# Loading the first token tile in two halves, its first weights on ScalarE's queue, and running its matmuls ahead of the second tile's

## The chip, the cores and the metric

The kernel runs on one core of a Trainium2 chip. The metric is the device time of one execution in microseconds (us). The profile is of one execution; a time of the kernel is the median of several runs without it. The core has TensorE (PE in the profile; its weight loads are PEld), VectorE (DVE), ScalarE (ACT), GpSimd (POOL) and SyncE (SP). SP and ACT issue the DMAs here, each into a queue of its own; the transfers of both queues run on the core's 16 DMA engines. In the trace a DMA is a short issue on SP or ACT, and it is over when its semaphore is full, which the profile calls its landing.

## The reference

Two attention blocks work on the same tokens x (2048 tokens of 1024 features, bfloat16), and a gate per token mixes them. Block A is linear attention with 32 heads of 32; block B is a dilated sliding window of 8 keys, 2 apart. Both project x with a 1024x3072 matrix, and both end in a 1024x1024 matrix.

```
g = sigmoid((x * gate_w).sum(-1))
a = A_ref(x, A_wqkv, A_wo)      # phi(q) (phi(k)^T v) / (phi(q) sum phi(k)), then @ wo
b = B_ref(x, B_wqkv, B_wo)      # softmax over 8 keys at distance 0, 2, .. 14, then @ wo
out = g * a + (1 - g) * b
```

What matters here is the first thing that the kernel computes: V of block B, that is x @ B_wqkv[:, 2048:3072].

## The kernel before, in words

The function plan() records every operation with P.op: its engine, an estimated cost, the tiles that it reads and writes, and a priority. P.schedule() then lays the operations out engine by engine with a small list scheduler (of what is ready, the lowest priority number first), and emit() writes each engine's instructions in that order, with semaphore waits where a dependence crosses engines or goes through a DMA. So a row's place in an engine's program is the planner's; on the chip each engine works through its rows in order, and one that waits holds up all behind it. plan() is run six times (PASSES), each time with the release times of the PSUM banks of the pass before, and the plan with the shortest estimated span is kept.

The tokens are cut in 16 tiles of 128. A token tile is needed transposed, features on the partitions: load_x (line 1334) issues one DMA transpose on SP for a tile, which fills xT[:, 0:8, tile], 8 groups of 128 features. The matmuls of a tile are 8 per half of V: each takes one feature group of the tile as its stationary operand (LDWEIGHTS reads xT) and streams 512 columns of the weights ws[0] past it, and the 8 add up in one PSUM bank. load_w (line 1339) loads a range d0 to d1 of the feature groups of one 512-column half of the weights: the first half comes in four pieces of two feature groups each, here called w0 to w3, of 256 KB each; the second half also comes in four pieces.

The V stage is written out in the list steps (lines 1417 to 1425). Each entry is (tile, half, first feature group, last). Before the change the first half goes

```
cuts = [(0, 4), (4, 6), (6, 8)] if half == 0 else [(0, 2), (2, 4), (4, 6), (6, 8)]
steps += [[(i, half, lo, hi) for i in range(2)] for lo, hi in cuts]
```

so tile 0 takes feature groups 0 to 3, then tile 1 the same ones, then both take 4 and 5, then both 6 and 7; tiles 2 and 3 follow whole; then the second half of the four tiles; then tiles 4 to 15, both halves of a feature group under one weight load (two, line 1363). group (line 1371) makes the matmuls of one entry. Where a group waits for a piece, all of PE waits. The results leave PSUM by move (line 1399) on ACT or DVE into one of 8 slots of vst, and SP stores them in HBM (line 1447).

Ahead of all this stand WARM small matmuls on constants into PSUM bank 7 (line 1410), which need no data and keep PE running while the first loads are under way.

Banks come from pools. In the V stage main holds banks 0 to 6. Then, at line 1472, main becomes banks 0 to 3, for all that follows until line 1824: K and Q of block B (lines 1605 to 1621: the first 1024 tokens, then the others) and the window attention, whose scores are in banks 4 to 7 and which starts when the first 1024 tokens of K and Q are done.

## Time and profile before

| what | value |
|---|---|
| median of 3 runs | 477.44 us (476.99 to 477.62) |
| the profiled execution | 477.52 us |
| its span in the profile | 475.7 us |
| PE busy in the span | 467.0 us, 98% |
| first matmul on data of the kernel | 6.20 us after the span's start |
| TensorE clock granted | 1.0 of full speed over the profile's slices |

The span is the time from the first to the last instruction in the profile; 1.8 us of the execution lie outside of it. PE is busy in all slices of the span, so time is read at PE: where its string of matmuls breaks, and what ended the break. At the start that is the arrival of x and of the weights. In the rows of instructions the first number is the start in us from the span's start, the second the time from the first start to the last end, xN the number of instructions in the row, and in square brackets the idle time of that engine ahead of it and what ended it.

### The profile page before, as it was taken

The numbers are of one execution on the slowest core, as the hardware profiler recorded it, in microseconds if no ns is written. First come the engines' busy times: TensorE is split into PE (matmuls) and PEld (weight loads), VectorE is DVE, ScalarE is ACT, GpSimd is POOL, SyncE is SP. The second block draws the span as 40 slices with busy tenths as digits, with TensorE's granted clock in tenths as the row PEclk, the third lists the DMA queues.
The fourth block names the chain that finished last, engine by engine and source line by source line (L and its number), as shares of the span: only waits on it lengthen the run. The fifth ranks groups of instructions, "written<-read, shape, count | busy, mean of one in ns | idle before, by whom it ended". The sixth has DMA issues, their size and how long they took to land.

```text
span 475.7 us, 9166 instructions
## 1 busy us (share of the span) xinstructions
PE 467.0 (98%) x3988; PEld 210.7 (44%) x3890; DVE 313.0 (66%) x554; ACT 130.1 (27%) x175; POOL 40.2 (8%) x39
## 2 busy tenths in 40 slices
PE   9999999999999999999999999999999999999997
PEld 2322244444445544454444544544444444444444
DVE  2121365799877888878864464589987777777522
ACT  2111112222243535556543423153221111111000
POOL 3000000000000000000068651010000000000000
PEclk9999999999999999999999999999999999999999
DMA  8999997332211253255325866671331111121111
GB/s 223 223 194 296 359 341 234 82 95 57 78 34 53 69 165 88 75 145 142 77 69 150 195 157 104 173 218 24 90 88 47 45 44 45 58 76 47 45 45 48
DMA packets 94969, 57.07 MB, mean 120 GB/s; under 512 B 55240, under 2 KB 88392, under 8 KB 94920
## 3 DMA queue, kind: packets, MB, share of 16 engines
q1 hardware_dynamic: 94088, 55.61, 43.6%
q10 hardware_dynamic: 832, 0.79, 0.6%
q8 instruction: 33, 0.54, 0.5%
q14 instruction: 16, 0.13, 0.1%
HBM read 30.56 MB, written 12.72 MB: 91 GB/s over the span
## 4 chain that ended last, share of the span: by engine, by line
PE 93%; DVE 3%; DMA 2%; issue 1%; POOL 0%; ACT 0%; DVEq 0%
PE ps_all L1375 46%; PE ps_all L1804 23%; PE ps_all L1733 11%; PE ps_all L1360 6%; PE ps_all L1366 4%; PE ps_all L1533 2%; PE ps_all L1560 1%; DMA z_hbm<-zc 1%; DMA zr<-z_hbm 1%; DVE p L1384 1%; DVE prod L1779 0%; DVE den L1780 0%; POOL zb L1687 0%; DVE kT L1402 0%; DVE pn L1784 0%
## 5 line engine op out<-in xcount | busy, mean ns | idle before, releaser
L1375 PE MATMUL ps_all<-xT,w 128*128 128x512 bf16 x500 | 110.2, 379 | 1.2 <-issue 0.8
L1375 PEld LDWEIGHTS ps_all<-xT,w 128*128 128x128 bf16 x512 | 49.6, 98 | 59.5 <-issue 0.3
L1381 ACT ACTIVATE e<-ps_all 128x512 bf16<-128x512 f32 x64 | 38.2, 597 | 125.1 <-PE ps_all L1375 116.2
L1375 PE MATMUL ps_all<-w,xT 128*128 128x512 bf16 x312 | 69.0, 379 | 1.1 <-DVE e L1382 1.0
L1804 PE MATMUL ps_all<-kT,aT 128*128 128x512 bf16 (+1 forms) x259 | 60.2, 372 | 0.3
L1804 PE MATMUL ps_all<-w,qT 128*128 128x512 bf16 (+1 forms) x255 | 59.7, 372 | 0.8 <-DVE p L1384 0.4
L1375 PE MATMUL ps_all<-kT,xT 128*128 128x512 bf16 x254 | 57.6, 379 | 0.3 <-issue 0.2
L1733 PE MATMUL ps_all<-pk,xn 128*128 128x512 bf16 x249 | 55.0, 379 | 1.1 <-issue 1.1
L1375 PEld LDWEIGHTS ps_all<-w,xT 128*128 128x128 bf16 x320 | 30.6, 98 | 41.5 <-DMA w<-in_B_wqkv_dram 5.5
L1405 DVE TENSOR_SCALAR o<-ps_all,gm 128x512 bf16<-128x512 f32 (+1 forms) x28 | 20.5, 732 | 28.1 <-PE ps_all L1804 27.6
L1804 PEld LDWEIGHTS ps_all<-w,qT 128*128 128x128 bf16 x264 | 25.7, 98 | 29.9 <-DVE p L1384 0.5
L1804 PEld LDWEIGHTS ps_all<-kT,aT 128*128 128x128 bf16 x264 | 25.8, 98 | 29.4
L1402 DVE CAST vst<-ps_all 128x512 bf16<-128x512 f32 x16 | 10.5, 690 | 42.8 <-PE ps_all L1360 31.5
L1375 PEld LDWEIGHTS ps_all<-kT,xT 128*128 128x128 bf16 x256 | 24.6, 98 | 29.9 <-issue 0.5
L1733 PEld LDWEIGHTS ps_all<-pk,xn 128*128 128x128 bf16 x256 | 24.5, 98 | 28.7
L1382 DVE TENSOR_SCALAR e<-e 128x512 bf16<-128x512 bf16 x64 | 18.8, 294 | 27.9 <-ACT e L1381 27.5
L1360 PE MATMUL ps_all<-w,xT 128*128 128x512 bf16 x96 | 36.4, 379 | 0.2
L1541 ACT ACTIVATE E<-ps_all 128x1824 bf16<-128x1824 f32 (+1 forms) x18 | 30.4, 1688 | 20.4 <-PE ps_all L1560 18.8
L1366 PE MATMUL ps_all<-w,xT 128*128 128x512 bf16 x92 | 34.9, 379 | 0.0
L1697 POOL TENSOR_TENSOR zacc<-zacc,pk 128x1024 f32<-128x1024 f32 x15 | 33.0, 2198 | 11.8 <-DVE E L1546 10.9
L1575 DVE TENSOR_TENSOR ao<-ps_all,rs 128x896 bf16<-128x896 f32 (+1 forms) x36 | 24.5, 684 | 0.2
L1403 ACT ACTIVATE kT<-ps_all 128x512 bf16<-128x512 f32 x26 | 15.0, 598 | 35.4 <-PE ps_all L1375 35.4
(69 smaller groups left out, 405.2 us busy)
## 6 DMA issues: line engine op xcount, KB each, us to landing
v<-vB_hbm SPq DMA_DIRECT2D x36, 132.0 KB, 3.2
vB_hbm<-vst SPq DMA_DIRECT2D x32, 132.0 KB, 6.3
w<-in_B_wqkv_dram SPq DMA_DIRECT2D x4, 1024.0 KB, 8.5
xt<-in_A_x_dram SPq DMA_DIRECT2D x16, 256.0 KB, 4.3
w<-in_A_wqkv_dram SPq DMA_DIRECT2D x4, 1024.0 KB, 9.3
xn<-in_A_x_dram SPq DMA_DIRECT2D x8, 512.0 KB, 4.9
out_dram<-o SPq DMA_DIRECT2D x15, 256.0 KB, 2.0
oB_hbm<-ao SPq DMA_DIRECT2D x32, 114.0 KB
```

Of the source, the lines that this page charges most:

```text
L1360: return e.add_instruction(mybir.InstMatmult(name=nc.get_next_instruction_name(), engine=mybir.EngineType.PE, ins=[e.lower_ap(rhs), e.lowe ...
L1366: e.matmul(bs[0].ap(), lhs(dc), rhs[0](dc), start=(dc == 0), stop=(dc == 7))
L1375: last = e.matmul(bank.ap(), lhs(dc), rhs(dc), start=(dc == 0), stop=(dc == 7))
L1381: P.op("act", lambda e: e.activation(e_[:, :], bank.ap(), ACT.Exp), act(512), reads=[bank.iv], writes=[e_.all()])
L1382: P.op("dve", lambda e: e.tensor_scalar(e_[:, :], e_[:, :], 1.0, 1e-6, op0=ALU.min, op1=ALU.add), 0.25, reads=[e_.all()], writes=[e_.all()])
L1403: fa = lambda e: e.activation(dst, src(), ACT.Copy)
L1405: fd = lambda e: e.tensor_scalar(dst, src(), scale, None, op0=ALU.mult)
L1541: P.op("act", lambda e: e.activation(E[:, 0:32 * nq].rearrange("p (j q) -> p j q", j=4), ps[:, 4:8, 0:8 * nq], ACT.Exp), act(32 * nq), rea ...
L1575: P.op("dve", lambda e, i0=i0, i1=i1, src=src: e.tensor_tensor(o_[:, :, i0:i1, :], src(0, 32), rs[:, :, i0:i1, None].to_broadcast([128, 2, ...
L1697: P.op("pool", lambda e, t=t: e.tensor_tensor(zacc[:, :], zacc[:, :], pkS[:, t, :], ALU.add), 2.2, reads=[src, zacc.all()], writes=[zacc.a ...
L1733: last = e.matmul(bank.ap(), tl[:, t, cs:cs + 128], pkS[:, t, r * 512:(r + 1) * 512], start=(t == 0), stop=(t == NT - 1))
L1804: last = e.matmul(bank.ap(0, f1 - f0), lh[:, k, t * 128:(t + 1) * 128], w[:, k, f0:f1], start=(first and k == 0), stop=(not first and k == 7))
```

## The change

Five things are edited in plan().

- The transpose of tile 0 is issued as two DMAs on SP: feature groups 0 to 3, then 4 to 7, each with its own semaphore. Tile 1 and all others are as before.
- The weight pieces w2 and w3 are issued on ACT's queue behind w0 and w1. Before, w0 and w1 were on ACT and w2 and w3 on SP, behind the transposes of tiles 0 and 1.
- In the first half of V, tile 0 goes through all of its 8 feature groups in four pieces of two, and tile 1 follows whole. A matmul group of tiles 0 to 3 now waits only for the feature groups of x that it reads.
- WARM goes from 50 to 40.
- The pool of four banks is set up at the second 1024 tokens of K and Q, so that K and Q of the first 1024 tokens have banks 0 to 6.

```diff
-    WARM = 50
+    WARM = 40
...
-        load_x(0, 0)
+        for i in range(2):
+            P.op("sp", lambda e, i=i: e.dma_start_transpose(xT[:, 4 * i:4 * i + 4, 0:128], x2[0, 0:128, 512 * i:512 * i + 512]),
+                 1.3, writes=[xT.part((4 * i, 4 * i + 4), (0, 128))], prio=0.01 * i, chan="x0_%d" % i, lat=0.7)
         load_x(1, 0.1)
         load_w(0, 0, Bw, 2048, 0.1, 0, 2, "act")
         load_w(0, 0, Bw, 2048, 0.2, 2, 4, "act")
-        load_w(0, 0, Bw, 2048, 0.3, 4, 6)
-        load_w(0, 0, Bw, 2048, 0.4, 6, 8)
+        load_w(0, 0, Bw, 2048, 0.3, 4, 6, "act")
+        load_w(0, 0, Bw, 2048, 0.4, 6, 8, "act")
...
-                    steps += [[(i, half, lo, hi) for i in range(2)] for lo, hi in cuts]
+                    if half == 0:
+                        steps += [[(0, 0, lo, lo + 2) for lo in range(0, 8, 2)], [(1, 0, 0, 8)]]
+                    else:
+                        steps += [[(i, half, lo, hi) for i in range(2)] for lo, hi in cuts]
...
-                o = group(bank, xs, w, [xr, ws[0].part((lo, hi), (half * 512, half * 512 + 512))], lo, hi)
+                o = group(bank, xs, w, [xT.part((lo, hi), (t * 128, (t + 1) * 128)), ws[0].part((lo, hi), (half * 512, half * 512 + 512))], lo, hi)
...
-        main = Pool(banks[0:4], soon)
         pending = []
...
         for e_ in range(2):
             if True:
+                if e_ == 1:
+                    main = Pool(banks[0:4], soon)
                 for j in range(8):
```

In what follows the built programs are listed engine by engine, instructions in their order, xN for N equal ones in a row. On PE, with the semaphores that each waits for: c_x1 is the load of token tile 1 (c_x0_0 and c_x0_1 the two halves of tile 0), c_w0_0_4 the piece of the weights' first half that begins at feature group 4. The piece w0 is c_w0_0_0, w1 is c_w0_0_2, w2 is c_w0_0_4 and w3 is c_w0_0_6. PE at the start of the V stage, before:

```order
2 L1360 MATMUL ps_all<-const-bfloat16-1.0 128x156 x49
3 L1375 MATMUL ps_all<-w_4_52,xT_49 128x512 [waits c_x0,c_w0_0_0,c_w0_0_2]
4 L1375 MATMUL ps_all<-w_4_52,xT_49 128x512 x3
5 L1375 MATMUL ps_all<-w_4_52,xT_49 128x512 [waits c_x1]
6 L1375 MATMUL ps_all<-w_4_52,xT_49 128x512 x3
7 L1375 MATMUL ps_all<-w_4_52,xT_49 128x512 [waits c_w0_0_4]
8 L1375 MATMUL ps_all<-w_4_52,xT_49 128x512 x3
9 L1375 MATMUL ps_all<-w_4_52,xT_49 128x512 [waits c_w0_0_6]
10 L1375 MATMUL ps_all<-w_4_52,xT_49 128x512 x3
11 L1375 MATMUL ps_all<-w_4_52,xT_49 128x512 [waits c_x2]
```

And the same place now:

```order
2 L1362 MATMUL ps_all<-const-bfloat16-1.0 128x156 x39
3 L1377 MATMUL ps_all<-w_4_52,xT_49 128x512 [waits c_x0_0,c_w0_0_0]
4 L1377 MATMUL ps_all<-w_4_52,xT_49 128x512
5 L1377 MATMUL ps_all<-w_4_52,xT_49 128x512 [waits c_w0_0_2]
6 L1377 MATMUL ps_all<-w_4_52,xT_49 128x512
7 L1377 MATMUL ps_all<-w_4_52,xT_49 128x512 [waits c_x0_1,c_w0_0_4]
8 L1377 MATMUL ps_all<-w_4_52,xT_49 128x512
9 L1377 MATMUL ps_all<-w_4_52,xT_49 128x512 [waits c_w0_0_6]
10 L1377 MATMUL ps_all<-w_4_52,xT_49 128x512
11 L1377 MATMUL ps_all<-w_4_52,xT_49 128x512 [waits c_x1]
12 L1377 MATMUL ps_all<-w_4_52,xT_49 128x512 x7
13 L1377 MATMUL ps_all<-w_4_52,xT_49 128x512 [waits c_x2]
```

The same 16 matmuls of tiles 0 and 1 stand ahead of the wait for tile 2. What moved is how many of them stand behind each wait: behind the wait for w3 there were 4, now there are 10, and tile 1 with its 8 stands last.

SP, its first rows before (w is the weights' pieces, xT the transposes, vB_hbm the stores of V):

```order
1 L1336 DMA_TRANSPOSE xT_49<-in_A_x_dram 128x8x128 x2
2 L1341 DMA w_4_52<-in_B_wqkv_dram 128x2x512 x2
3 L1336 DMA_TRANSPOSE xT_49<-in_A_x_dram 128x8x128 x2
4 L1341 DMA w_4_52<-in_B_wqkv_dram 128x2x512 x4
5 L1336 DMA_TRANSPOSE xT_49<-in_A_x_dram 128x8x128 x2
```

SP now:

```order
1 L1346 DMA_TRANSPOSE xT_49<-in_A_x_dram 128x4x128 x2
2 L1336 DMA_TRANSPOSE xT_49<-in_A_x_dram 128x8x128 x3
3 L1341 DMA w_4_52<-in_B_wqkv_dram 128x2x512 x4
4 L1336 DMA_TRANSPOSE xT_49<-in_A_x_dram 128x8x128 x2
```

The two weight pieces are gone from between tile 1 and tile 2; on ACT the row of the pieces goes from x2 to x4, ahead of ACT's first read of PSUM. SP then issues one transpose more (the half) and two weight pieces fewer.

Further on, PE's order is the same in both programs to the end. SP, DVE and ACT stand in another order up to the first scores of the window attention, and the same from there on. SP in the second part of the V stage before (vst stores of tiles 7 to 11 between loads of 1 MB halves of later weights, the gate's vector gw and the gate's rows xt):

```order
25 L1341 DMA w_6_54<-in_B_wqkv_dram 128x8x512
26 L1447 DMA vB_hbm<-vst_80 128x528 x2
27 L1341 DMA w_5_53<-in_B_wqkv_dram 128x8x512
28 L1447 DMA vB_hbm<-vst_80 128x528 x2
29 L1341 DMA w_6_54<-in_B_wqkv_dram 128x8x512
30 L1447 DMA vB_hbm<-vst_80 128x528 x2
31 L1455 DMA gw_99<-in_gate_w_dram 128x1024
```

And now:

```order
22 L1341 DMA w_6_54<-in_B_wqkv_dram 128x8x512
23 L1341 DMA w_5_53<-in_B_wqkv_dram 128x8x512
24 L1452 DMA vB_hbm<-vst_80 128x528 x2
25 L1460 DMA gw_99<-in_gate_w_dram 128x1024
26 L1452 DMA vB_hbm<-vst_80 128x528 x2
27 L1464 DMA xt_47_95<-in_A_x_dram 128x1024
28 L1464 DMA xt_48_96<-in_A_x_dram 128x1024
29 L1464 DMA xt_49_97<-in_A_x_dram 128x1024
30 L1341 DMA w_6_54<-in_B_wqkv_dram 128x8x512
```

A third load of 1 MB now stands ahead of the stores of tile 8, and the gate's loads have come forward.

## The prediction

> **What bounds the kernel now.** I read the page's first part and the chain of work that ended last, then PE's idle time through the whole span, and then the first 10 us row by row.
>
> ```profile
> PE 467.0 (98%) x3988; PEld 210.7 (44%) x3890; DVE 313.0 (66%) x554; ACT 130.1 (27%) x175; POOL 40.2 (8%) x39
> PE 93%; DVE 3%; DMA 2%; issue 1%; POOL 0%; ACT 0%; DVEq 0%
> 70.95 10.74 PE ps_all L1375 x49
> 81.74 10.74 PE ps_all L1375 x49
> ```
>
> PE is busy for 467.0 of 475.7 us and carries 93% of the chain. The last two rows are from the chain in the part that computes K and Q: two equal pieces start 10.79 us apart, and PE does nothing else between. So the kernel is one string of matmuls from the first on data to the end, and a time saved or lost at its head is saved or lost at its end, as long as nothing behind comes to be waited for. The question is when the string begins, and whether it breaks in the first microseconds. PE there, from the rows in order of time, and the weight loads (PEld), whose brackets tell what each row waited for:
>
> ```profile
> 0.93 3.55 PE L1360 MATMUL ps_all<-const-bfloat16-1.0 128*128 128x156 bf16 x26
> 4.18 1.89 PE L1360 MATMUL ps_all<-const-bfloat16-1.0 128*128 128x156 bf16 x24
> 5.96 1.42 PEld L1375 LDWEIGHTS ps_all<-w,xT 128*128 128x128 bf16 x8 [5.04 <-DMA w<-in_B_wqkv_dram]
> 7.67 0.57 PEld L1375 LDWEIGHTS ps_all<-w,xT 128*128 128x128 bf16 x4 [0.29 <-DMA w<-in_B_wqkv_dram]
> 8.46 0.65 PEld L1375 LDWEIGHTS ps_all<-w,xT 128*128 128x128 bf16 x4 [0.22 <-DMA w<-in_B_wqkv_dram]
> 6.20 10.74 PE ps_all L1375 x49
> 16.99 2.97 PE ps_all L1375 x13
> 19.96 0.22 PE ps_all L1366
> ```
>
> The warm-up runs until 6.07, the first data is there at 5.96, and the first real matmul starts at 6.20. From there 64 matmuls (4 tiles, 2 halves, 8 each) take until 19.96: 13.76 / 64 = 0.215 us each, with no hole in it. The waits of 0.29 and 0.22 us at 7.67 and 8.46 are those of the weight loads, which run ahead of the matmuls; each piece came just as it was needed. The warm-up and the loads thus end within 0.3 us of each other, and the first 16 matmuls (tiles 0 and 1) end at 6.20 + 16 x 0.215 = 9.64. That is the number to compare, since behind it PE's order is unchanged.
>
> **When the loads land.** The issue start and the time to landing, for each load by itself (in turn tile 0, both ACT pieces w0 and w1, tile 1, w2, w3, tile 2):
>
> ```profile
> L1336 SPq DMA_TRANSPOSE xT<-in_A_x_dram x1: 1352/1352/1352, 0.8 to 0.8; - x1
> DMA to landing us min/median/max: 5.0/5.0/5.0
> L1341 ACTq DMA_DIRECT2D w<-in_B_wqkv_dram x2: 446/466/487, 0.8 to 1.3; - x2
> DMA to landing us min/median/max: 2.9/3.6/4.3
> L1336 SPq DMA_TRANSPOSE xT<-in_A_x_dram x1: 1486/1486/1486, 2.2 to 2.2; - x1
> DMA to landing us min/median/max: 4.2/4.2/4.2
> L1341 SPq DMA_DIRECT2D w<-in_B_wqkv_dram x1: 573/573/573, 3.8 to 3.8; - x1
> DMA to landing us min/median/max: 3.9/3.9/3.9
> L1341 SPq DMA_DIRECT2D w<-in_B_wqkv_dram x1: 464/464/464, 4.4 to 4.4; - x1
> DMA to landing us min/median/max: 4.0/4.0/4.0
> L1336 SPq DMA_TRANSPOSE xT<-in_A_x_dram x1: 1232/1232/1232, 4.9 to 4.9; - x1
> DMA to landing us min/median/max: 4.5/4.5/4.5
> ```
>
> So tile 0 lands at 5.8, w0 at 3.7, w1 at 5.6, tile 1 at 6.4, w2 at 7.7, w3 at 8.4, tile 2 at 9.4. Is it the issue that holds them back, or the transfer? Stretches of the first 8 us; the last two numbers are the busy share of the DMA engines and GB/s:
>
> ```profile
> 0.00:2.00 2.00, 1.16 (x10) 0.11 (x1) 0.96 (x2) 1.19 (x1) 1.37 (x10) 1.00 0.00 1
> 2.00:3.00 1.00, 1.00 (x10) 0.00 (x0) 0.38 (x7) 0.09 (x1) 0.19 (x1) 1.00 0.72 220
> 3.00:4.00 1.00, 1.00 (x10) 0.00 (x0) 0.41 (x3) 0.00 (x0) 0.64 (x4) 1.00 1.12 267
> 4.00:5.00 1.00, 1.00 (x14) 0.00 (x0) 0.44 (x2) 0.00 (x0) 0.90 (x4) 1.00 1.15 338
> 5.00:6.00 1.00, 1.00 (x16) 0.04 (x2) 0.05 (x1) 0.00 (x0) 0.90 (x6) 1.00 1.28 282
> 6.00:7.00 1.00, 0.87 (x6) 0.47 (x6) 0.52 (x3) 0.00 (x0) 0.25 (x2) 1.00 0.93 306
> 7.00:8.00 1.00, 1.00 (x7) 0.41 (x5) 0.00 (x0) 0.00 (x0) 0.00 (x0) 1.00 1.40 286
> ```
>
> Nothing moves before 2 us, and from 3 us on the engines are full (packets overlap, so the share passes 1), at 267 to 338 GB/s. The six pieces of 256 KB that tiles 0 and 1 need, 6 x 0.262 = 1.57 MB, are through when the column adds up to that: 0.22 by 3, 0.49 by 4, 0.83 by 5, 1.11 by 6, 1.41 by 7, 1.57 by 7.55 us. The last of them lands 0.85 us behind that, at 8.4; tile 1, the fourth, landed at 6.4, 0.6 us behind the 1.05 MB of four pieces at 5.8. **The stream, not the issue, sets the last landing.**
>
> **The change, part by part.**
>
> Ten warm-up matmuls less. Within the second row above the starts run from 4.18 to 6.07 - 0.23 = 5.84, 23 steps of 0.072; ten of them are 0.72 us. The last would start at 5.12, so the first real matmul could start at 5.19. This bounds the gain of the whole change: 6.20 - 5.19 = 1.0 us. The slow ones (0.13 us apart, first row) all stay.
>
> Tile 0 in two halves. The trace has no transpose of a half tile. Its issue costs between 0.68 (half of 1.352) and 1.35 us (all of it). The first matmuls need the first half and w0, which is there at 3.7. If its landing at 5.8 moves in proportion to its bytes it is some 0.5 us earlier, about 5.3; if it waits for w1 as now, there is no gain; if it lands beside w0, it is in time for 5.19. I take 5.2 to 5.3 for the start. The other half and w1 come by the 1.05 MB less tile 1, before 6.
>
> Two weight pieces on ACT. ACT's two issues took 0.45 and 0.49 us; two more end near 2.8, and ACT's next row waits for PE anyway (its first read of PSUM comes when a group ends, at 9.2 before), so nothing is queued behind them. On SP 2 x 0.5 us of issues go, and one transpose issue more comes, so tile 1 is issued between 2.2 and 3.5 and tile 2 between 3.7 and 5.0, against 4.9: tile 2 is not issued later than before by more than 0.1 us. It lands at 9.4 at the latest, where it is needed at 9.64 or later in all but the fastest case.
>
> The order of the matmuls. Here stands the price. Before, 4 matmuls were left behind the last of the six pieces; now 8 are left if tile 1 is last, 10 if w3 is. With the first stretch filled a little better (220 to 290 GB/s between 2 and 3 us, which saves at most 0.25 us) the six pieces are through at 7.3 to 7.55, and the last lands 0.6 to 0.85 us behind, at 7.9 to 8.4.
> - Tile 1 last (0.6, as tile 1 before): landing at 7.9 to 8.15, eight matmuls of 0.215 = 1.72, end at 9.65 to 9.9. Against 9.64: +0.0 to +0.25 us.
> - w3 last: ten matmuls, 2.15; landing at 7.9 to 8.4 gives an end at 10.05 to 10.55, +0.4 to +0.9.
> - Neither bound, since the pieces come as needed: start at 5.19, end at 8.63, -1.0 us, and tile 2 must then land by 8.6.
>
> I take the first, since w3's issue ends near 2.8 and tile 1's 0.7 us later at the least, at 3.5: +0.1 us, from the middle of its 0.0 to 0.25.
>
> The Trainium skill, "DMA: Bandwidth & Descriptors", section "Issuing engines are not separate DMA queues", states that DMAs begun by different engines run on the same 16 DMA engines and interleave, and that using several issuers saves only issue time. By it the move to ACT's queue gives nothing in a full stream and the sum stays at the order's +0.1; without it, by issue times alone, w3 would land some 2 us earlier and the gain would be the 1.0 us. The busy shares above agree with the rule.
>
> The pool of seven banks in the first half of K and Q. PE has no hole there (the pieces of 10.74 us), so more banks cannot give PE time: 0. The banks 4 to 6 that the scores need later are used up to five groups before the first scores; a group is 8 x 0.215 = 1.7 us, a bank is emptied in 0.6 to 0.7 us, so the scores find them free. What hides the new order on DVE and ACT is PE's string; where that cover could go is SP's order in the second part of the V stage:
>
> ```profile
> L1447 SPq DMA_DIRECT2D vB_hbm<-vst x1: 3572/3572/3572, 38.7 to 38.7; - x1
> DMA to landing us min/median/max: 10.0/10.0/10.0
> 51.08 1.09 ACT L1403 ACTIVATE vst<-ps_all 128x512 bf16<-128x512 f32 x2 [5.82 <-PE ps_all L1360]
> ```
>
> The store of tile 8 lands at 48.7, and ACT writes the same vst slot again at 51.08, when PE has done tile 12. With 1 MB more ahead of that store, at some 340 GB/s 3.1 us, it lands at 51.8 and ACT waits 0.7 us. PE goes on: it holds 7 banks, and five are left beside the two that wait. Cost 0; if the delay passed the 5 x 1.7 = 8.6 us of those banks, PE would stop.
>
> Sum: 477.52 (the profiled execution) + 0.1 = 477.6, and 0.08 less against the median of 477.44: 477.5.
>
> **Rivals.** What a measurement of this kernel can tell from no change is about 0.2%, 0.95 us.
> - *The pieces arrive as needed.* The halves and the early issue let PE start at 5.19 and run through: -0.6 to -1.0 us, 476.4 to 476.8. For it: w0 lands at 3.7 alone, so a single small load is quick; the first 2 us move nothing. Against it: the engines are full from 3 us on.
> - *w3 is late* (the other side). Before, w2 and w3 were ahead of tile 2 in one queue; now they share the engines with the transposes from another. w1 shows what that can mean: issued at 1.3, beside tile 0's transpose, it took 4.3 us against w0's 2.9. If the transposes go first, w3 lands at 8.4 as now, ten matmuls behind it: 10.55, +0.9, 478.4; if tile 2 too goes ahead of it, at 9.4, +1.9, 479.4. It decides from a landing of w3 after 8.4.
> - *The new order of SP, ACT or DVE stops PE later*, by stores or the gate's loads: +1 to +3 us.
> - *Nothing moves*: start earlier, but the string breaks by the same amount; this is my forecast but for 0.1 us.
>
> **How the numbers follow.** Forecast (tile 1 or w3 last within the stream): 0.40, its own range -0.4 to +0.9 us. The pieces as needed: 0.25, of which 0.18 beyond 0.95 us with the runs' scatter (476.99 to 477.62). w3 late: 0.27, of which 0.21 beyond 0.95. A later stop: 0.08. Faster 0.18, slower 0.21 + 0.08 = 0.29, within 0.2% the rest, 0.53. The range reaches from 476.4, where the whole gain is taken in, to 478.7, past w3 landing as late as now.
>
> **What would show it.** The first real matmul between 5.2 and 5.6; then holes in PE ahead of the wait for w3 or for tile 1, in sum some 0.9 us, and the end of the 16th matmul near 9.7; no hole from there on. Wrong, if the 16th ends before 9.0 or after 10.5, if the DMA stream carries more than 340 GB/s between 2 and 7 us, or if PE waits for a PSUM bank later.

## The result, and the profile after

| what | before | after |
|---|---|---|
| median | 477.33 us (476.99 to 477.62, 4 runs) | 480.65 us (479.70 to 481.50, 4 runs) |
| ratio | | 1.0054, 95% interval 1.0037 to 1.0071 |
| the profiled execution | 477.52 us | 481.50 us |
| its span | 475.7 us | 479.8 us |

The changed kernel is slower, by 1.8 to 3.4 us. 477.5 was forecast, within 476.4 to 478.7.

PE at the start, in rows in order of time; behind the three rows of matmuls stand two of the weight loads. Lines have moved: L1362 is the warm-up's, L1377 the matmuls', L1346 the half transposes', L1336 still the whole ones'.

```profile
0.92 5.28 PE L1362 MATMUL ps_all<-const-bfloat16-1.0 128*128 128x156 bf16 x39
6.00 1.19 PE L1377 MATMUL ps_all<-w,xT 128*128 128x512 bf16 x4
9.23 14.80 PE L1377 MATMUL ps_all<-w,xT 128*128 128x512 bf16 x60 [2.04 <-DMA xT<-in_A_x_dram]
10.43 0.15 PEld L1377 LDWEIGHTS ps_all<-w,xT 128*128 128x128 bf16 x1 [0.28 <-issue]
10.86 0.15 PEld L1377 LDWEIGHTS ps_all<-w,xT 128*128 128x128 bf16 x1 [0.28 <-issue]
```

Four matmuls start at 6.00, and then PE stands still for 2.04 us, until a transfer into xT. The chain of work that ended last says which: the one issued second, tile 0's feature groups 4 to 7.

```profile
0.81 1.30 SPq L1346
2.11 0.06 issue
2.17 6.93 DMA xT<-in_A_x_dram
9.09 0.14 issue
9.23 14.80 PE ps_all L1377 x60
24.02 0.22 PE ps_all L1368
```

It lands at 2.17 + 6.93 = 9.1 us. The string that before was at L1366 (here L1368) at 19.96 is there at 24.02, 4.06 us later. The first scores of the window attention, at about 125 us, show the same distance, 129.28 against 125.22, and so do the spans, 479.8 - 475.7 = 4.1:

```profile
125.22 0.60 PE L1533 MATMUL ps_all<-qx,kT 64*64 64x114 bf16 x32
129.28 0.60 PE L1537 MATMUL ps_all<-qx,kT 64*64 64x114 bf16 x32
```

The first row is of the kernel before, the second of the changed one. So the whole loss of this execution lies in the first 24 us, and nothing behind costs or gains. Two things make it up; the stretches of 4 to 14 us show both (the column behind POOL is the TensorE clock granted, then the DMA engines' busy share and GB/s):

```profile
4.00:5.00 1.00, 1.00 (x10) 0.00 (x0) 0.44 (x2) 0.00 (x0) 0.90 (x4) 1.00 1.03 293
5.00:6.00 1.00, 1.00 (x11) 0.13 (x2) 0.05 (x1) 0.00 (x0) 0.89 (x6) 1.00 1.56 161
6.00:7.00 1.00, 1.00 (x6) 0.34 (x4) 0.51 (x3) 0.00 (x0) 0.25 (x2) 1.00 0.79 105
7.00:8.00 1.00, 0.18 (x1) 0.00 (x0) 0.00 (x0) 0.00 (x0) 0.00 (x0) 1.00 1.05 192
8.00:9.00 1.00, 0.00 (x0) 0.00 (x0) 0.00 (x0) 0.00 (x0) 0.00 (x0) 1.00 1.24 227
9.00:10.00 1.00, 0.77 (x3) 0.32 (x4) 0.00 (x0) 0.00 (x0) 0.00 (x0) 0.86 1.28 287
10.00:12.00 2.00, 2.00 (x6) 0.76 (x5) 0.00 (x0) 0.60 (x1) 0.00 (x0) 0.50 1.03 173
12.00:14.00 2.00, 2.00 (x8) 0.81 (x7) 0.30 (x1) 0.00 (x0) 0.00 (x0) 0.71 0.86 270
```

*The stream.* From 5 to 8 us the DMA engines are about as busy as before (the three shares add up to 3.40, before to 3.61), but move 161, 105 and 192 GB/s where they moved 282, 306 and 286. The pieces come late with it:

```profile
L1336 SPq DMA_TRANSPOSE xT<-in_A_x_dram x1: 1302/1302/1302, 3.5 to 3.5; - x1
DMA to landing us min/median/max: 6.3/6.3/6.3
L1341 ACTq DMA_DIRECT2D w<-in_B_wqkv_dram x2: 491/522/552, 1.8 to 2.4; - x2
DMA to landing us min/median/max: 5.6/6.1/6.6
0.81 2.61 SPq L1346 DMA_TRANSPOSE xT<-in_A_x_dram  x2
3.47 6.49 SPq L1336 DMA_TRANSPOSE xT<-in_A_x_dram  x3
```

Tile 1 lands at 3.5 + 6.3 = 9.8 us, w2 at 1.8 + 5.6 = 7.4, w3 at 2.4 + 6.6 = 9.0. The last two rows are SP's own: two half transposes take 2.61 us to issue, 1.30 and 1.26, nearly as long as a whole one each (1.35 before); and the three behind them take 6.49.

*The clock.* In this execution the granted clock falls to half soon after PE is running again. The weight loads of the first fence are 0.43 us apart, twice 0.215. From the clock column the fall lasts (0.14 x 1 + 0.5 x 2 + 0.29 x 2) / 0.5 = 3.4 us and takes 0.14 + 1.0 + 0.58 = 1.7 us of full clock. The same 60 matmuls took 13.11 us in a later execution that kept its clock (e4 below), against 14.80 here: 1.7 again. The other 2.4 of the 4.06 us come from 12 matmuls standing behind 9.23: 9.23 + 12 x 0.216 = 11.8 at full clock, against 9.44 before.

That 9.44 is 0.2 us less than the 9.64 of the prediction, because the string before began at 5.99 and not at 6.20. Its next string starts here:

```profile
19.80 0.38 PE L1366 MATMUL ps_all<-w,xT 128*128 128x512 bf16 x1
```

From 6.20 to 19.80 there is room for 63 matmuls 0.216 us apart, and 64 stand there; 62 of them have a record, and the 6.20 is the second's. The other executions of the changed kernel had a mean granted clock of 0.999 or 1.0 and took 479.70 to 480.79 us.

### The profile page after: what moved, and what is told of

It is laid out like the page before. It is cut to its first block, busy times and chain, and to the rows that moved or that the text cites. A ratio compares the mean times of both kernels' runs of the same rounds, so it can differ in the third digit from the quotient of the medians.

```text
span 479.8 us, 9206 instructions
## 1 busy us (share of the span) xinstructions
PE 474.0 (99%) x4025; PEld 211.5 (44%) x3890; DVE 314.2 (65%) x555; ACT 129.5 (27%) x174; POOL 40.2 (8%) x39
## 4 chain that ended last, share of the span: by engine, by line
PE 91%; DMA 4%; DVE 3%; POOL 0%; ACT 0%; SPq 0%; issue 0%; DVEq 0%
PE ps_all L1377 46%; PE ps_all L1810 23%; PE ps_all L1739 9%; PE ps_all L1368 4%; PE ps_all L1362 4%; PE ps_all L1537 2%; DMA xT<-in_A_x_dram 1%; PE ps_all L1564 1%; DMA z_hbm<-zc 1%; DMA zt<-zlo 1%; DVE p L1386 1%; DMA zr<-z_hbm 1%; DVE prod L1785 0%; DVE den L1786 0%; DVE zs L1688 0%; POOL zb L1693 0%
## 5 line engine op out<-in xcount | busy, mean ns | idle before, releaser
L1377 PE MATMUL ps_all<-xT,w 128*128 128x512 bf16 x512 | 111.7, 379 | 0.0
L1377 PEld LDWEIGHTS ps_all<-xT,w 128*128 128x128 bf16 x512 | 49.6, 98 | 59.4 <-issue 0.3
L1377 PE MATMUL ps_all<-w,xT 128*128 128x512 bf16 x320 | 72.6, 386 | 2.0 <-DMA xT<-in_A_x_dram 2.0
L1810 PE MATMUL ps_all<-w,qT 128*128 128x512 bf16 (+1 forms) x264 | 60.7, 373 | 0.2 <-DVE p L1386 0.2
L1377 PE MATMUL ps_all<-kT,xT 128*128 128x512 bf16 x256 | 58.1, 379 | 0.0
L1739 PE MATMUL ps_all<-pk,xn 128*128 128x512 bf16 x256 | 56.6, 379 | 0.0
L1377 PEld LDWEIGHTS ps_all<-w,xT 128*128 128x128 bf16 x320 | 31.3, 100 | 44.9 <-issue 9.6
L1404 DVE CAST vst<-ps_all 128x512 bf16<-128x512 f32 x16 | 10.5, 690 | 44.6 <-PE ps_all L1362 29.2
L1377 PEld LDWEIGHTS ps_all<-kT,xT 128*128 128x128 bf16 x256 | 24.6, 98 | 29.9 <-issue 0.5
L1368 PE MATMUL ps_all<-w,xT 128*128 128x512 bf16 x96 | 36.4, 379 | 0.0
L1362 PE MATMUL ps_all<-w,xT 128*128 128x512 bf16 x96 | 36.4, 379 | 0.0
L1703 POOL TENSOR_TENSOR zacc<-zacc,pk 128x1024 f32<-128x1024 f32 x15 | 33.0, 2198 | 11.8 <-DVE E L1550 10.9
```

The costliest lines, as they stand in the source:

```text
L1362: return e.add_instruction(mybir.InstMatmult(name=nc.get_next_instruction_name(), engine=mybir.EngineType.PE, ins=[e.lower_ap(rhs), e.lowe ...
L1368: e.matmul(bs[0].ap(), lhs(dc), rhs[0](dc), start=(dc == 0), stop=(dc == 7))
L1377: last = e.matmul(bank.ap(), lhs(dc), rhs(dc), start=(dc == 0), stop=(dc == 7))
L1703: P.op("pool", lambda e, t=t: e.tensor_tensor(zacc[:, :], zacc[:, :], pkS[:, t, :], ALU.add), 2.2, reads=[src, zacc.all()], writes=[zacc.a ...
L1739: last = e.matmul(bank.ap(), tl[:, t, cs:cs + 128], pkS[:, t, r * 512:(r + 1) * 512], start=(t == 0), stop=(t == NT - 1))
L1810: last = e.matmul(bank.ap(0, f1 - f0), lh[:, k, t * 128:(t + 1) * 128], w[:, k, f0:f1], start=(first and k == 0), stop=(not first and k == 7))
```

## The experiments

Each ratio is to the kernel before on the same chip in the same session; its medians there were 478.03 (e1 to e4), 478.08 (e5 to e8), 477.77 (e9 to e12) and 477.55 us (e13, e14).

| run | what it is | median us | ratio, 95% interval | clock fell in |
|---|---|---|---|---|
| e1 | after, w2 and w3 back on SP | 479.98 | 1.0041 (1.0026 to 1.0056) | 1 of 8 |
| e2 | after, tile 0 in one transpose | 481.68 | 1.0071 (1.0040 to 1.0101) | 1 of 5 |
| e3 | before, w2 and w3 on ACT | 482.35 | 1.0107 (1.0072 to 1.0141) | 1 of 4 |
| e4 | after, nothing changed | 479.78 | 1.0047 (1.0029 to 1.0064) | 1 of 10 |
| e5 | before, halves only | 479.02 | 1.0018 (1.0006 to 1.0030) | 0 of 10 |
| e6 | before, order only | 478.60 | 1.0013 (0.9999 to 1.0027) | 0 of 10 |
| e7 | after, order of before | 480.62 | 1.0052 (1.0030 to 1.0074) | 2 of 5 |
| e8 | before, 40 warm-ups and the pool | 478.51 | 1.0011 (0.9999 to 1.0024) | 0 of 10 |
| e9 | before, w2 and w3 on ACT, later | 480.92 | 1.0076 (1.0052 to 1.0100) | 3 of 6 |
| e10 | before, w2 alone on ACT | 478.12 | 1.0008 (0.9997 to 1.0018) | 0 of 10 |
| e11 | after, hole filled | 479.45 | 1.0032 (1.0019 to 1.0044) | 0 of 8 |
| e12 | after, w2 and w3 on ACT, later | 484.84 | 1.0162 (1.0140 to 1.0185) | 4 of 4 |
| e13 | as e9, orders held | 477.89 | 1.0003 (0.9990 to 1.0017) | 0 of 10 |
| e14 | before, w2 and w3 early on SP | 478.28 | 1.0013 (1.0000 to 1.0026) | 0 of 10 |

The last column counts executions whose mean granted clock was 0.996 or less, which is 3.4 us at half speed in 480.

### e1 to e4: one part undone or alone

e4 is the changed kernel once more, for comparison on the same chip. The others, shortened:

```diff
e1, on the changed kernel:
-        load_w(0, 0, Bw, 2048, 0.3, 4, 6, "act")
-        load_w(0, 0, Bw, 2048, 0.4, 6, 8, "act")
+        load_w(0, 0, Bw, 2048, 0.3, 4, 6)
+        load_w(0, 0, Bw, 2048, 0.4, 6, 8)
e2, on the changed kernel:
-        for i in range(2):
-            P.op("sp", lambda e, i=i: e.dma_start_transpose(xT[:, 4 * i:4 * i + 4, 0:128], x2[0, 0:128, 512 * i:512 * i + 512]),
-                 1.3, writes=[xT.part((4 * i, 4 * i + 4), (0, 128))], prio=0.01 * i, chan="x0_%d" % i, lat=0.7)
+        load_x(0, 0)
e3, on the kernel before:
-        load_w(0, 0, Bw, 2048, 0.3, 4, 6)
-        load_w(0, 0, Bw, 2048, 0.4, 6, 8)
+        load_w(0, 0, Bw, 2048, 0.3, 4, 6, "act")
+        load_w(0, 0, Bw, 2048, 0.4, 6, 8, "act")
```

> The changed kernel with w2 and w3 back on SP, behind the transposes of tiles 0 and 1; all else as changed. Theory Q (the weight pieces on the second queue hold up the second half of tile 0): the half lands before 6 us, the hole of 2.2 us at 7.0 to 9.2 is gone, the clock stays at 1.0, and the time is within 1 us of before (476.4 to 478.4). Theory H (two half transposes cost SP a whole issue more, and the half itself is slow): the second half still lands at 8 us or later, and the time stays 2 to 3.5 us above before. Theory O (tile 1 last in the order of matmuls): the hole moves to the wait for w3 or tile 1 and stays above 1.5 us.

> The changed kernel with tile 0 loaded by one transpose, as before; w2 and w3 stay on ACT's queue. Theory Q: whichever transpose is under way beside w2 and w3 is held up, now tile 1: tile 1 lands at 8.5 us or later against 6.4, PE has a hole of 1 us or more ahead of it, and the time is 1 to 3 us above before. Theory H: tile 0 lands at 5.8, tile 1 at about 6.5 and w3 by 8, no hole above 0.7 us, and the time is within 1 us of before. Theory O: 0.5 to 1.5 us above before, with the hole ahead of w3 or tile 1.

> The kernel before with w2 and w3 on ACT's queue and nothing else of the change. Theory Q: the DMA rate between 5 and 8 us falls from 282 to 306 GB/s to below 200, tile 1 lands after 8 us against 6.4, and the time is 1 to 3 us above before. Theory H and theory O: nothing moves by more than 0.5 us.

> The changed kernel once more. If the late landing of the second half of tile 0 (9.1 us) is the kernel's and not that one execution's, it lands after 8 us again and PE has a hole of 1.5 us or more ahead of the fifth matmul; the time is 479.7 to 481.5. The low clock of 0.5 between 9.7 and 13.1 us may be there or not: theory C says that it follows the hole in some executions, costs 1.7 us there, and makes the spread between 479.7 and 481.5; without it the span is 478 to 479.

In e4 the second half of tile 0 lands late again, at 2.2 + 6.7 = 8.9 us, with a hole of 1.42 us and at full clock:

```profile
8.99 12.25 PE L1377 MATMUL ps_all<-w,xT 128*128 128x512 bf16 x56 [1.42 <-DMA xT<-in_A_x_dram]
```

So the late half is the kernel's, and not one execution's. e3 is the clearest: nothing but the queue of two pieces is edited, and it has the highest median of the four. With the pieces gone from SP, tile 2's transpose moves up too, from 4.9 to 3.6 us. e3's chain, and the packets of 6 to 10 us by queue (q1 is SP's, q10 ACT's; packets, MB, and the time they took as a share of 16 engines) beside those of the kernel before:

```profile
2.21 8.22 DMA xT<-in_A_x_dram
10.43 0.05 issue
10.47 13.12 PE ps_all L1375 x60
```

```profile
q1 hardware_dynamic: 1273, 0.32, 84.2%
q10 hardware_dynamic: 275, 0.26, 40.8%
```

```profile
q1 hardware_dynamic: 2639, 1.03, 114.1%
```

The middle fence is e3, the last the kernel before. Tile 1, issued at 2.21 as before, lands at 10.43 instead of 6.4. The packets take 125% of the engines' time for 0.58 MB; before they took 114% for 1.03 MB. Each byte takes about twice the time in this stretch, in which both queues have work.

But e1, which takes just this part back, is not faster than the changed kernel (479.98 against 479.78 of e4). Its weight loads, and SP:

```profile
8.82 0.11 PEld L1377 LDWEIGHTS ps_all<-w,xT 128*128 128x128 bf16 x2 [2.28 <-DMA w<-in_B_wqkv_dram]
9.54 2.49 PEld L1377 LDWEIGHTS ps_all<-w,xT 128*128 128x128 bf16 x13 [0.60 <-DMA w<-in_B_wqkv_dram]
4.81 1.09 SPq L1341 DMA_DIRECT2D w<-in_B_wqkv_dram  x2
```

The pieces are on SP behind three transposes of 1.3 us each, so they are issued at 4.81 and 5.4 instead of 3.75 and 4.37, and land at 8.8 and 9.5. PE waits for them with tile 1 there (7.1) and unused, since tile 1's matmuls stand behind tile 0's. e2 says what the halves are worth in the changed kernel: without them it is 1.9 us slower still in the medians, though the two intervals overlap. PE stands still twice there, 1.97 us for tile 0, which lands at 0.81 + 6.0 = 6.8 instead of 5.8, and 2.27 us for w3, which lands at 2.36 + 8.30 = 10.66:

```profile
10.70 10.53 PE L1375 MATMUL ps_all<-w,xT 128*128 128x512 bf16 x48 [2.27 <-DMA w<-in_B_wqkv_dram]
```

So in e2 PE waits for a piece on ACT's queue, with ten matmuls behind it; tile 1 lands as late, at 2.2 + 8.5 = 10.7.

### e5 to e8: each other part alone

```diff
e5, on the kernel before (all shortened):
-        load_x(0, 0)
+        for i in range(2):
+            P.op("sp", lambda e, i=i: e.dma_start_transpose(xT[:, 4 * i:4 * i + 4, 0:128], x2[0, 0:128, 512 * i:512 * i + 512]),
+                 1.3, writes=[xT.part((4 * i, 4 * i + 4), (0, 128))], prio=0.01 * i, chan="x0_%d" % i, lat=0.7)
e6, on the kernel before:
-                    steps += [[(i, half, lo, hi) for i in range(2)] for lo, hi in cuts]
+                    if half == 0:
+                        steps += [[(0, 0, lo, lo + 2) for lo in range(0, 8, 2)], [(1, 0, 0, 8)]]
+                    else:
+                        steps += [[(i, half, lo, hi) for i in range(2)] for lo, hi in cuts]
e7, on the changed kernel: the same lines the other way round
e8, on the kernel before:
-    WARM = 50
+    WARM = 40
...
-        main = Pool(banks[0:4], soon)
...
+                if e_ == 1:
+                    main = Pool(banks[0:4], soon)
```

> The kernel before, with nothing changed but tile 0's transpose cut in two: 50 warm-ups, the last two weight pieces on SP's queue and the order of matmuls all as before. Theory H (a half costs SP a whole issue): SP spends 3 x 1.30 us on transposes ahead of the weight pieces, which are issued at 4.8 and 5.4 us instead of 3.75 and 4.37, so they land near 8.8 and 9.5 as in the run with the pieces back on SP, against 7.6 and 8.4 before; tile 1 fills the time till 7.9, then a hole of about 0.9 us ahead of the third piece: +1.0 us in the span, some 479.0 against 478.0 of the kernel before on this chip. If a half costs only half an issue, or the stream and not the issue sets the landings, no difference.

> The kernel before, with nothing changed but the order of the first 16 matmuls (tile 0's eight, two by two, and then tile 1's eight); the loads are as before. Theory O (the order takes away the work that covers the weight pieces): the pieces land at 7.6 and 8.4 us as before, tile 0's fifth and seventh matmuls wait for them with 0.65 and 0.4 us of hole, and tile 1's eight end at 10.6 instead of 9.64: +1.0 us, about 479.0 against 478.0. If the order is harmless, 478.0 and no hole of PE between 6 and 20 us.

> The changed kernel with the order of matmuls of the kernel before; halves, all four pieces on ACT's queue, 40 warm-ups and the moved pool stay. With the loads as in the changed kernel the second half and tile 1 land near 9.0 and 9.7. If the loads alone are the cause, tile 1's first four matmuls now wait till 9.7 and 12 matmuls stand behind that: the 16th ends near 12.3, against 11.7 in the undisturbed run of the changed kernel, so +0.6 us on it (about 480.4 where the changed kernel has 479.8). If the order is the larger part of the loss, it is faster than the changed kernel, near 479.

> The kernel before, with 40 warm-ups instead of 50 and the pool of banks built anew only at the second pass, nothing else. Both were put at a cost of nothing. The first real matmul then starts when tile 0 has landed, at 5.85 + 0.13 us, at most 0.2 us earlier: 477.8 to 478.0 and a granted clock of 1.0. If ten warm-ups fewer make the clock fall or come late, +1.5 us or more, with the rows of the windows from 6 to 14 us at 0.5.

The halves alone cost 0.06 to 0.30%, 0.9 us in the medians, as theory H said. The rows show two places. PE starts later, since its first group waits for both halves here, and the second lands at 2.2 + 4.2 = 6.4 where the whole tile landed at 5.8; and the weight loads wait longer (the two pieces on SP land at 4.8 + 3.7 = 8.5 and 5.4 + 3.8 = 9.2):

```profile
6.85 3.64 PE L1377 MATMUL ps_all<-w,xT 128*128 128x512 bf16 x15 [0.99 <-DMA xT<-in_A_x_dram]
8.58 0.55 PEld L1377 LDWEIGHTS ps_all<-w,xT 128*128 128x128 bf16 x4 [0.56 <-DMA w<-in_B_wqkv_dram]
9.29 0.70 PEld L1377 LDWEIGHTS ps_all<-w,xT 128*128 128x128 bf16 x4 [0.16 <-DMA w<-in_B_wqkv_dram]
10.69 1.19 PEld L1377 LDWEIGHTS ps_all<-w,xT 128*128 128x128 bf16 x7 [0.70 <-DMA xT<-in_A_x_dram]
```

The order alone is put at +0.5 us by the medians, with an interval that just reaches no change. In its trace the weight loads wait longer for the same pieces, 0.50 and 0.66 us, where they waited 0.29 and 0.22 before:

```profile
7.68 0.11 PEld L1375 LDWEIGHTS ps_all<-w,xT 128*128 128x128 bf16 x2 [0.50 <-DMA w<-in_B_wqkv_dram]
8.45 3.57 PEld L1375 LDWEIGHTS ps_all<-w,xT 128*128 128x128 bf16 x18 [0.66 <-DMA w<-in_B_wqkv_dram]
```

e7 shows no difference, under the changed kernel's loads, between the two orders (480.62 against 479.78 in another session, ratios 1.0052 and 1.0047): there is no other work to put in the hole, since tile 1, at 3.5 + 6.2 = 9.7, is later still than the second half, at 2.2 + 6.7 = 8.9. e8 gained nothing from fewer warm-ups and the moved pool, and lost nothing that can be told.

The parts do not add up. Alone they cost 0.9, 0.5, 4.3 and 0.4 us in the medians, in sum 6; together 1.8 (e4) to 3.3. As the rows read, the halves and the new order let PE begin and go on with tile 0 alone, which softens what the queue does, and the queue takes two issues from SP, which softens what the halves do; no run shows that by itself.

### e9 to e12: the hand-over, its amount, and the hole

```diff
e9, on the kernel before; e12, the same on the changed kernel (shortened):
-        load_w(0, 0, Bw, 2048, 0.1, 0, 2, "act")
+        w01 = load_w(0, 0, Bw, 2048, 0.1, 0, 2, "act")
...
+        load_w(0, 0, Bw, 2048, 0.3, 4, 6, "act", after=[w01])
+        load_w(0, 0, Bw, 2048, 0.4, 6, 8, "act", after=[w01])
e10, on the kernel before:
-        load_w(0, 0, Bw, 2048, 0.3, 4, 6)
+        load_w(0, 0, Bw, 2048, 0.3, 4, 6, "act")
e11, on the changed kernel:
+            if (t, half, lo) == (0, 0, 2):
+                def cover(e):
+                    for k in range(24):
+                        last = same(e, banks[7].ap(0, 156), one(128), one(156), True, True) if k else e.matmul(banks[7].ap(0, 156), one(128), one(156), start=True, stop=True)
+                    return last
+                P.op("pe", cover, 24 * mm(156), writes=[banks[7].iv], after=[o])
```

> The kernel before with the last two weight pieces on ScalarE's queue, issued only once the first piece has landed (near 3.7 and 4.3 us, the times at which SP issued them before) instead of at 1.8 and 2.4 us. Theory Q1 (what is issued earlier is moved earlier: with four pieces handed over by 2.9 us, tile 1's transpose stands behind them): tile 1 lands at 6.4 us again, the pieces at 7.6 to 8.5, 478.0 to 478.8. Theory Q2 (copies on a second queue and transposes slow each other whenever they run side by side): a landing past 9 us again for the pieces or tile 2, a rate under 200 GB/s between 5 and 8 us, and 480 or more.

> The kernel before with one weight piece (features 4 and 5) moved to ScalarE's queue and the last one left on SP's. If each piece of 256 KB that is handed over ahead of tile 1's transpose holds it up alike, tile 1 lands half as late as with two pieces, near 8.4 us (6.4 before, 10.4 with two): the fifth matmul waits from 7.1 to 8.5, +1.4 to 1.8 us, about 479.7. If one piece is free and only the second costs: 478.0 to 478.4.

> The changed kernel with 24 more matmuls of ones (24 x 0.066 = 1.6 us at full clock) behind the first four real ones, in the hole ahead of the late half. Theory C (the clock falls to half for 3.4 us where PE has stood still for about 2 us): no execution shows a granted clock below 0.999, against roughly one in five of the kernels with such a hole so far (8 of 36), and none lies 2 us above the others; the median stays at that of the changed kernel, 479.8, or up to 0.2 us above where the late half lands early. If the fall has another cause, one in five still shows 0.996.

> The changed kernel with its last two weight pieces issued on ScalarE's queue only once the first has landed, as in the run of the kernel before with that. By Q1 the second half lands near 6.1 and tile 1 near 7.1, the pieces at 7.6 to 8.8, and what is left is the cost of the halves and of the order: +1.0 to 1.3 us, 479.1 to 479.4. By Q2: as the changed kernel, 479.8 or more.

e9 and e12 cannot be read as times of what they were made for. The wait moved the planner's estimate of w3, and it laid out other orders: SP issues all of the first four transposes ahead, and PE has a group of V's second half ahead of the wait for w3. In e9, the three rows that wait for a piece behind w1:

```
7 L1375 MATMUL ps_all<-w_4_52,xT_49 128x512 [waits c_w0_0_4]
9 L1375 MATMUL ps_all<-w_4_52,xT_49 128x512 [waits c_w0_1_0]
11 L1375 MATMUL ps_all<-w_4_52,xT_49 128x512 [waits c_w0_0_6]
```

c_w0_1_0 is issued late, on SP, and PE waits 2.95 us for it in e9 and 3.74 us in e12. Their landings still tell something: in e9 tile 1 is on time again (2.2 + 4.3 = 6.5), while w3, issued at 4.1, takes 6.0 us.

e10 missed its expectation on the good side. One piece on ACT's queue costs nothing that can be told, tile 1 lands at 2.2 + 5.3 = 7.5, not 8.4, and the packets of 6 to 10 us run at the old speed, 1.10 MB in 123%:

```profile
q1 hardware_dynamic: 3493, 1.10, 122.9%
q10 hardware_dynamic: 17, 0.00, 0.4%
```

So the cost is not so much per piece; it comes with the second piece, or with what moves up on SP when that piece leaves it (tile 2's transpose is issued at 4.3 here, at 3.6 in e3).

e11 leaves out nothing; its additional matmuls write a bank that is not read. PE's rows:

```profile
6.83 1.02 PE L1377 MATMUL ps_all<-w,xT 128*128 128x512 bf16 x4 [0.80 <-DMA xT<-in_A_x_dram]
7.76 1.76 PE L1362 MATMUL ps_all<-const-bfloat16-1.0 128*128 128x156 bf16 x23
9.71 11.60 PE L1377 MATMUL ps_all<-w,xT 128*128 128x512 bf16 x52 [0.19 <-issue]
```

With the hole filled, none of 8 executions shows the fall. That alone would be weak: where PE has a hole of about 2 to 3 us (the changed kernel, e1 to e4, e7, e9) it fell in 10 of 42, so 8 without one could be chance, with (32/42)^8 = 0.11. But the size of the hole goes with it through all runs. In e12, with holes of 0.75 and 3.74 us, the clock fell in 4 of 4. In e5, e6, e8, e10, e13 and e14, none of whose profiles shows a hole over 1 us once the matmuls run, in 0 of 60.

The traces also tell when. They hold a record of the clock (e9's is empty) that begins with the first full clock; in the kernel before that is at 4.31 us, where its warm-ups go from 0.13 to 0.07 us apart (the clock column shows 1.00 ahead of it too, for want of a record). In the changed kernel's profile it begins at 6.32 us, in e7's at 6.60, in e12's at 5.27; the clock falls at 9.73, 10.01 and 12.10, which is 3.41, 3.41 and 2 x 3.41 us later. In the last 3.41 us ahead of the fall PE stood still for 2.04, 2.27 and 3.37 us. Counted in the same stretches of 3.41 us from the first full clock, PE stands still for at most 1.93 us in any stretch of the profiles of e1 to e4, which keep their clock, although e3's hole is 2.71 us long: it lies across two stretches. So in these seven profiles a fall hangs on how much of one stretch a hole fills, and the first full clock comes at another time in each execution.

### e13 and e14: early, or on the second queue

Two explanations were left for the queue: what is handed over early goes first, or a second queue slows the stream. e13 is e9 with the orders held (every later issue on SP waits for w1, each of PE's V groups follows the one before it in the list, the stores of V come behind the weights). e14 hands both pieces over nearly as early, at 2.2 and 2.8 us where e3 has 1.8 and 2.4, but on SP's own queue; PE's order follows the loads there, tile 0's eight matmuls and then tile 1's.

```diff
e13, on the kernel before, beside e9's lines (shortened):
+        P.held_up = load_w(0, 0, Bw, 2048, 0.2, 2, 4, "act")
...
+        if eng == "sp" and self.held_up:
+            o.deps.add(self.held_up)
...
+            if t < 4:
+                o.deps.update(before)
+                before = [o]
e14, on the kernel before:
-        load_w(0, 0, Bw, 2048, 0.3, 4, 6)
-        load_w(0, 0, Bw, 2048, 0.4, 6, 8)
+        load_w(0, 0, Bw, 2048, 0.05, 4, 6)
+        load_w(0, 0, Bw, 2048, 0.06, 6, 8)
```

> The kernel before with the last two weight pieces on ScalarE's queue, issued once the first has landed (3.7 and 4.1 us), as in the earlier run of that kind, but with the order of matmuls of the kernel before held, and with SP's next transposes issued only once the second piece has landed (near 5.7 us, 4.9 before). Theory Q1 (only the early hand-over holds up tile 1): tile 1 lands at 6.4 to 6.6 us, the pieces at 7.6 and 8.5, tile 2 near 9.9; PE waits 0.3 us at most for tile 2: 478.0 to 478.5. Theory Q2 (two pieces on a second queue beside transposes slow the stream whenever they are issued): the fourth piece or tile 2 lands past 10.3 us, under 200 GB/s in some microsecond between 6 and 10, +1 us or more.

> The kernel before with the last two weight pieces ahead of tile 1's transpose, all on SP's own queue (issued near 2.2 and 2.8 us, the transpose near 3.3); the order of matmuls follows them: tile 0's eight first, then tile 1's. No second queue carries more than before. Q1: what is handed over ahead is moved ahead: the pieces land near 6.5 to 7.5, tile 1 at 8.4 or later; if the order of hand-over is all that there is to the loss, tile 1 lands as late as 10 us and PE stands still for 2 us or more: 480 or more. Q2 (the stream slows only where both queues carry much): all six transfers are through by 8.5 us as before and no microsecond between 5 and 8 is under 250 GB/s; tile 1's eight matmuls start near 8.0 to 8.5 and the 16th ends at 10.0 to 10.3, +0.4 to 0.7 us: 478.4 to 478.8.

Neither is slow. In e13 both pieces are on ACT's queue, and they land at 3.8 + 3.8 = 7.6 and 4.2 + 4.4 = 8.6, tile 1 at 2.2 + 4.4 = 6.6; the ratio is 1.0003. In e14 both are handed over by 3.3 us, and all six transfers are through by 8.0; its stretches of 5 to 8 us, where e3 had 289, 122 and 147 GB/s:

```profile
5.00:6.00 1.00, 1.00 (x10) 0.00 (x0) 0.06 (x1) 0.00 (x0) 0.90 (x6) 1.00 1.08 316
6.00:7.00 1.00, 1.00 (x11) 0.00 (x0) 0.43 (x2) 0.00 (x0) 0.26 (x2) 1.00 1.19 309
7.00:8.00 1.00, 1.00 (x9) 0.52 (x6) 0.09 (x1) 0.00 (x0) 0.00 (x0) 1.00 1.28 278
```

```profile
6.00:7.00 1.00, 1.00 (x14) 0.20 (x3) 0.44 (x3) 0.00 (x0) 0.25 (x2) 1.00 1.11 122
7.00:8.00 1.00, 0.77 (x4) 0.15 (x2) 0.07 (x1) 0.00 (x0) 0.00 (x0) 1.00 1.20 147
```

The second fence is e3. So early alone is not the cause, and two pieces on the second queue alone are not either, in the form in which e13 has them: it also holds tile 2's transpose back to 5.9 us. What the kernels with the slow stream share is that pieces of ACT's queue and the transposes of two tiles or parts of tiles are under way side by side: w2 and w3 beside tile 1 and tile 2 in e3, beside tile 0's second half and tile 1 in the changed kernel, w3 beside tiles 2 and 3 in e9. In all of them a third transpose is handed over by 3.7 us, in the kernel before, e10, e13 and e14 at 4.3 or later. e1 and e5 hand one over at 3.5 without the two pieces; their rate is low only from 5 to 6 us (156 and 119 GB/s). No run varied the third transpose by itself, and why a byte then takes twice as long is open.

A slow stretch does not even need the second queue. In e13 SP's queue alone has packets between 9 and 10 us, 0.12 MB in 110.8% of the engines' time, while tiles 2 and 3 are under way:

```profile
9.00:10.00 1.00, 1.00 (x6) 0.39 (x4) 0.00 (x0) 0.16 (x1) 0.00 (x0) 1.00 1.11 116
```

That is the rate under 200 GB/s that theory Q2 named as its sign. It costs nothing there: tile 2 lands at 5.9 + 4.2 = 10.1, and PE's string has no hole.

The Trainium skill, "DMA: Bandwidth & Descriptors", section "Queues, rings and completion order", states that a DMA engine goes round robin between the queues that have work, a packet from each in turn. Whether that is at work here no run shows: in e3 the two queues moved 1273 and 275 packets, 0.32 and 0.26 MB, between 6 and 10 us, and the profile does not tell what one turn is. That taking turns would make both slower, the page does not state either.

No version came out ahead of the kernel before. Its own string has no hole, and w2, w3 and tile 2 come hardly ahead of their matmuls: the weight loads that waited for them start at 7.67, 8.46 and 9.41, the 9th, 13th and 17th matmul at 7.71, 8.58 and 9.44. So an earlier start alone, with these loads, could gain no more than 0.1 us.

## Why the prediction was wrong

- **"The other half and w1 come by the 1.05 MB less tile 1, before 6."** This is the step that failed. w1 landed at 5.1, but the other half at 9.1 (8.9 in e4), and 12 matmuls stand behind it: 9.23 + 12 x 0.216 = 11.8 for the end of the 16th at full clock, which was put at 9.65 to 9.9. The working counted the megabytes ahead of the half and took the rate of the kernel before for granted; that the move of w2 and w3 lowers the rate, e3 shows, and why it does is open.
- **"The stream, not the issue, sets the last landing."** Right of the kernel before, and carried over wrongly in two ways. The stream is not fixed: it fell to 105 to 192 GB/s at the same busy share (e3: half the bytes per busy time). And with the queue put back the issue does set the landing: in e1 and e5 w2 and w3 land about 1 us late because SP issues them 1.06 us later, behind one more transpose.
- **Two weight pieces on ACT.** ACT itself was right: its issues end near 2.9 and nothing waits on it. What the move does to the transposes was priced at nothing; alone it costs 0.7 to 1.4% (e3).
- **Tile 0 in two halves.** In the profiled execution the first half landed at 0.81 + 4.5 = 5.3, as worked out, but that was luck: it landed at 5.9 in e1, 6.1 in e5, 6.2 in e7 and e12, 6.4 in e4 and 6.7 in e11, no earlier than the whole tile before (5.8). An issue costs nearly a whole transpose's, 1.30 us, the upper of the two bounds; the sum let tile 2 bear it, but with the pieces on SP they bear it.
- **Ten warm-ups less.** The first real matmul started at 6.00, not at 5.2 to 5.3; before it was 5.99, so the bound of 1.0 us for the gain was 0.8. In this execution nearly all of the 39 warm-ups ran at 0.13 us (5.28 us in all; 49 took 5.14 before), so that fewer of them saved nothing. e8 tells the same: its first real matmul starts at 6.00 too. The working took the moment at which the warm-ups become fast for fixed; the traces have it between 3.5 us (e2) and 6.8 (e14).
- **The order.** +0.1 us was forecast for all; alone it is at 0.5 us (0.0 to 1.3), by the holes ahead of w2 and w3 that tile 1 no longer fills. Tile 1 landed last, as forecast, but at 9.8, and PE's wait was for tile 0's second half.
- **The pool and the later order of SP, DVE and ACT**: 0, and nothing else shows. The distance to the kernel before is 4.06 us at 20 us, at 125 us and at the end.
- **The rivals.** The nearest was *w3 is late*: an ACT piece beside transposes, decided by a landing after 8.4. w3 landed at 9.0; but its price of at most +1.9 us was for w3 alone, and PE waited for a transpose in the other queue. In e2, with tile 0 whole, w3 is what PE waits for, till 10.66. No rival let the stream itself slow, and none had the clock: a hole at the start was priced by its length, and in one execution of four or so it costs 1.7 us more.
- **The rule of the Trainium skill**, "DMA: Bandwidth & Descriptors", section "Issuing engines are not separate DMA queues", by which the move gives nothing: it gave nothing. That it could take something away, neither the rule nor the sum said.

Of the signs that were named for a wrong prediction, one is there: the 16th matmul ends after 10.5 us (at 11.8 even without the fall of the clock), and the hole ahead of tile 0's second half is 2.04 us, where holes of 0.9 us ahead of w3 or tile 1 were expected.

## What to carry to other kernels

A queue moved to another engine changes what runs side by side, not just who issues: before counting bytes at the old rate, ask which transfers will now be under way together, and give a slower stream a rival of its own. A DMA transpose cut in two cost nearly two whole issues, and everything behind it on its queue pays for the second. Where PE's first microseconds hang on several loads, keep an order in which another tile's matmuls can fill the wait for a late piece.

## What the runs showed of the hardware that was not expected

- A transpose of half a tile takes nearly as long to issue as one of a whole tile: 1.30 and 1.26 us (2.61 for two) against 1.35.
- Two queues that have work at once can move half the bytes in the same busy time: 0.58 MB in 125% (e3) against 1.03 MB in 114% of the engines' time between 6 and 10 us. One queue can be slow too: 0.12 MB in 110.8% of the engines' time in 1 us (e13). SP's issues stretch with it: three transposes took 6.49 us.
- TensorE's clock can fall to half behind a hole of about 2 us, for 3.4 us, in some executions and not in others (10 of 42, and 4 of 4 behind 3.7 us); in the profiles it fell 3.41 or 2 x 3.41 us behind the first full clock. The Trainium skill, "TensorE: Matmul & The Clock Gate", section "Part 1: The HAM clock gate", states a free-running window of 3413 ns after which an idle array gets half its clock; the length of the fall agrees, and so do these distances. The advice of the same page, section "Why this matters for your kernels", to keep idle gaps under some 3 us is too generous here: 2.04 us was enough.
- The warm-up ends at another time in each execution: with the same 49 matmuls at 5.7 (e9) to 7.2 us (e14), since they go from 0.13 to 0.07 us apart early or late:

```profile
0.93 4.79 PE L1360 MATMUL ps_all<-const-bfloat16-1.0 128*128 128x156 bf16 x49
```

```profile
0.93 6.15 PE L1360 MATMUL ps_all<-const-bfloat16-1.0 128*128 128x156 bf16 x49
7.13 13.76 PE L1375 MATMUL ps_all<-w,xT 128*128 128x512 bf16 x62
```

The first is e9, the others e10, whose string begins 0.9 us later than the kernel before's and has no hole. This alone moves an execution by up to a microsecond, and is a part of the scatter of all these times (476.79 to 479.67 for the kernel before).
